# Two layers of attention and Fourier mixing: who issues layer 1's swap transfers, and where VectorE's small tasks stand

## The chip, the cores and the metric

One core of a Trainium2 chip runs the whole program as one launch. The core has a matrix engine (TensorE, PE in the profile, with its weight loads as PEld), a vector engine (VectorE, DVE), an engine for functions of one operand (ScalarE, ACT), a general one (GpSimd, POOL), and one that only issues transfers (SyncE, SP). Each engine takes its instructions in the order in which the program writes them, and waits on semaphores for the others. Matrix results land in PSUM, which has eight banks of 128 x 512 floats.

The metric is the device time in microseconds of one execution. Before the change it was 2400.1 us, the median of three runs (2399.7 to 2401.8).

## The reference

All arrays are float32, with S = 2048 tokens, D = 640 and 32 heads of 20. Two layers follow each other, and each is an attention block and a Fourier block, both with a residual:

```python
def _A_ref(x, wqkv, wo):
    qkv = (x @ wqkv).reshape(B, S, 3, H, Dh).transpose(2, 0, 3, 1, 4)
    q, k, v = qkv[0], qkv[1], qkv[2]
    p = softmax(einsum("bhqd,bhkd->bhqk", q, k) * Dh ** -0.5)
    o = einsum("bhqk,bhkd->bhqd", p, v)
    return o.transpose(0, 2, 1, 3).reshape(B, S, D) @ wo

def _B_ref(x, seq_re, seq_im, hid_re, hid_im):
    a = einsum("bsd,ed->bse", x, hid_re)
    b = einsum("bsd,ed->bse", x, hid_im)
    return einsum("ts,bse->bte", seq_re, a) - einsum("ts,bse->bte", seq_im, b)

x = x + _A_ref(layernorm(x), wqkv, wo)
x = x + _B_ref(layernorm(x), ...)
x = x + _A_ref(layernorm(x), wqkv, wo)     # the same weights again
x = x + _B_ref(layernorm(x), ...)
```

## The kernel before

**Precision.** A float32 product is made of three matmuls in a shorter format: an operand is split into a high part (a copy, rounded) and a low part (the value minus the high part), and high x high, high x low and low x high are added. So every operand costs two elementwise operations: `split` gives the copy to ScalarE (line 93) or VectorE (line 91) and the subtraction to VectorE (line 94).

**The stages of a layer.** A prologue (`Qkv.prologue`, line 370) normalizes the tokens, turns them so that the hidden dimension lies on the partitions, and computes the first chunk of 128 query and of 128 key columns and half of the values, block by block: four blocks (tb) of 512 tokens. Then attention runs over 512 steps (8 groups of four heads, 4 query blocks, 16 key tiles); a step is two score tiles of 128 x 1024, their exponentials, and the products with the values. The other eight chunks of q and k and the other half of the values are computed inside attention, by the generator `work` (line 502). An output projection and the Fourier block end the layer; the end of layer 0's Fourier block is interleaved with the beginning of layer 1's prologue. Whether the layer is the second is what `s.given` says.

**Turning the tokens.** Blocks 0 and 1 are turned by TensorE (`turn`, line 189). Blocks 2 and 3 go another way. `spaced` (line 216) lets ScalarE write the normalized tokens in an order of 4 groups. `swap` (line 225) then lets VectorE transpose each group in squares of 32 x 32 into a tile of its own (line 229, 4 operations, tensor name xz), and 16 transfers (line 232, xs<-xz) bring the squares to their partitions: transfer i of group g reads group g's transposed tile and writes 32 partitions of slab i. The first eight (g = 0, 1) are issued by SyncE, the others by GpSimd. `unspaced` (line 234) splits the result for the matmuls, the copies on ScalarE (xt, line 93). `swap(2)` stands at the end of block 0's work, behind the two `spaced` and ahead of block 1's chunk; `swap(3)` stands in block 1's value tiles, behind the third of four.

**A block of the prologue**, in the program's order: one q chunk and one k chunk, 15 matmuls each (line 111, pqk<-xt,wqk), each followed by `keep` (line 256), where ScalarE makes the high part (hl) and the Square (sq) for a bound on the scores (line 294), VectorE the low part (line 297), and GpSimd stores both to DRAM (line 265); then the matmul of `norms` over the Square of q (line 306, pn<-sq); then four value tiles of 15 matmuls (pv), each evicted by ScalarE (`own`, line 339). Between the value tiles stand the normalizing of the next tokens and `unspaced` of the next block. PSUM's banks go round: `Qkv.bank` (line 185) adds one to `s.n` and takes bank `s.n % 8`. The four value tiles of the last block are the last use before attention lays out its banks anew: three score tiles of two banks each (banks 0 to 5), one bank for the chunks that are still to come and one for the sum over values.

**The order inside attention** is written out by hand as strings. While `work` has chunks left and the step is below 233, a burst of 8 steps follows `DENSE` (line 585). Its letters: s, a score tile and its exponential by ScalarE from PSUM; d, a score tile that VectorE first copies to SBUF (line 688), with its exponential from there; v, the value products of one step; f, a part of a chunk (8 of its 15 matmuls, and at the next f the other 7); n, the norm's matmul of the chunk that is done; h, one place for a small VectorE task. Each of the sixteen value tiles has a shorter string of 4 steps without h.

A place h runs one task of the first of these lists that has any (`step`, line 665): `soon` (what `keep` left: the high part, the low part, the squares; and, when a chunk has had its last block, the next chunk's weights), `ends` (the five operations that finish an accumulator and store it), `held`, and else one task of the constants' comparison. `settle` empties a list at once. The comparison (`Check`, line 988) reads the Fourier matrices through GpSimd's transfers (cq) and checks their symmetries on VectorE, some 26 loads and 200 tasks a layer; `compare` (line 892) hands its tasks out at a pace that runs with the steps, and lets `s.landed` steps pass behind each load before the first task that reads it. All of a layer's comparisons must be out by step 448.

**The weights of the next chunk.** The function `following` (line 522) makes the high and the low part of the next chunk's weights (lines 91 and 94, wqk<-wraw) and fetches the raw weights of the chunk behind it. It is appended to `soon` when the norm's matmul of the chunk's last block is issued, and line 793 settles `soon` there and then inside a burst.

Of the kernel before, what the change touches and what calls it, by code (L numbers as in the profile page):

```python
# [5 lines left out]
F32 = mybir.dt.float32  # L6
F32R = mybir.dt.float32r
# [3 lines left out]
OP = mybir.AluOpType  # L11
# [8 lines left out]
ND = D // 128  # L20
NT = S // 128
NB = S // 512
# [20 lines left out]
def mha_fnet_kernel(ctx, tc, x_in, wqk, wv, wo, seq, hid, nat_seq, nat_hid, out):  # L43
# [107 lines left out]
    class Qkv:  # L151
# [73 lines left out]
        def swap(s, tb):  # L225

            zs = [s.vals(f"v{NT - 1 - g}", [ND * 128], F32, "xz") for g in range(4)]
            for g, z in enumerate(zs):
                V.transpose(z, s.y[tb][:, g].rearrange("p c n f -> p (c n f)"))
            for g, z in enumerate(zs):  # L230
                for i in range(4):
                    (nc.sync if g < 2 else G).dma_start(s.y[tb][32 * g:32 * g + 32, i].rearrange("p c n f -> p (c n f)"), z[32 * i:32 * i + 32])

        def unspaced(s, tb):

# [134 lines left out]
        def prologue(s, vals, xt, fill, att):  # L370
# [42 lines left out]

            def own(tb, n, between=None):
                t = 4 * tb + n
                p = s.bank([128, HD], "pv")
                for dc in range(ND):
                    for f in s.value(p, t, dc):
                        f()
                    if between and dc == 1:  # L420
                        between()
                s.own(p, t, 0, False)
# [79 lines left out]
        def work(s):  # L502

            order = [ND + 1, 1, ND + 2, 2, ND + 3, 3, ND + 4, 4]
            w = {0: s.w1}

            def chunk(i):
                c = order[i]
                for tb in range(NB):
                    p = bank("fill", [128, 512], "pqk")  # L510
                    for more in pieces([s.product(p, w[i], tb, dc) for dc in range(ND)], 8 if (i, tb) < (5, 1) else 5):
                        if more:
                            yield True
                    sq = s.keep(p, c, tb, True, s.fill)

                    def after():
                        s.norms(lambda *a: bank("fill", *a), c, tb, sq)
                        s.made.add((c, tb))
                        if tb == NB - 1:
                            s.made.add(c)  # L520

                            def following():
                                if i + 1 < len(order):
                                    w[i + 1] = s.weights(s.fill("w", [2, ND, 128], F32R, "wqk"), order[i + 1], True)
                                if i + 2 < len(order):
                                    s.fetch(order[i + 2])

                            if s.defer is None:
                                following()
                            else:  # L530
                                s.defer.append(following)
                    yield after

            for i in range(4):
                yield from chunk(i)
            for t in range(NT):
                p = bank("fill", [128, HD], "pv")
                for more in pieces([s.value(p, t, dc) for dc in range(ND)], 15):
                    if more:
                        yield True  # L540
                s.own(p, t, 1, True)
                yield None
            s.made.add("v")
            for i in range(4, 8):
                yield from chunk(i)

            s.silent = True
            r = s.bounds()
            ok = const.tile([128, 1], F32, name="ok", bufs=2)
            V.tensor_scalar(ok[:H], r[:H, 2:3], (GUARD / SCALE) ** 2, None, op0=OP.is_le)  # L550

            def after():
                p = bank("fill", [1, 1], "pok")
                PE.matmul(p, ok[:H], one[:H], start=True, stop=True)
                V.tensor_scalar(s.flag, p, float(H), None, op0=OP.is_equal)
            yield after
# [25 lines left out]
    class Attention:  # L582
        THIN = 233
        LAST = range(448, 512, 16)
        DENSE = "ssdfhhhhsshhsvhvhssvhvssdfhhhhsshhsvhvhssnvv"
        ENDING = "sDsvDhhsfssdvhvssdhvhvsDhsfsDsvhhvsDsvhvsDhsvhvsDhsfsDsvhvhshDshvvv"
        LOOSE = range(THIN, THIN + 176, 16)
        STRING = "sDhsfsDshvvshDsvvshDsfDhsvvsDsvvsDsfshDshvhvsDsvvshDsvhhvsDsnvhv"
# [157 lines left out]
        def sweep(s, shift, begin, fill=lambda n: None, plan=None, block=None, compare=lambda n: None, norm=None):  # L746
# [20 lines left out]
            while n < len(s.steps):  # L767
                opened(n)
                order = plan and plan(n)
                if order:  # L770

                    while done < n - 1:
                        s.values(done)
                        done += 1
                    t, loose = 2 * n, "h" in order
                    for k, c in enumerate(order):
                        if c in "sdD":
                            m, j = divmod(t, 2)
                            if not j and m > n:
                                opened(m)  # L780
                            s.scores(m, j, c)
                            if j and not loose:
                                s.held.append(lambda m=m: compare(m))
                            t += 1
                        elif c == "v":
                            s.values(done)
                            done += 1
                        elif c == "h":
                            s.step(lambda: compare(t // 2 - 1, True))
                        else:  # L790
                            (block if c == "f" else norm if loose else fill)(t // 2)
                            if c == "n" and n < s.THIN:
                                s.settle()
                        if not loose and k + 1 < len(order) and "d" not in order[k + 1:k + 3]:
                            release()
                    n = t // 2
                    continue
                release()
                s.scores(n, 0)
                s.scores(n, 1)  # L800
                more, owed = fill(n) and n >= 2 and n + 1 < len(s.steps), n - 1 - done
                compare(n)
                n += 1
                if plan and n <= s.THIN:
                    count = owed + 1
                elif more and owed < 3:
                    calm = n + 1
                    continue
                else:
                    count = min(owed, 1)  # L810
                    if owed > 1 and (done + 1) % NT and n > calm:
                        calm = n + 1
                        count = 2
                for _ in range(count):
                    s.values(done)
                    done += 1
# [5 lines left out]
        def run(s, done, project, check):  # L822
# [69 lines left out]
            def compare(n, one=False):  # L892
# [4 lines left out]
                for _ in range(1 if one else 2):  # L897
# [2 lines left out]
                        break  # L900
                    task = later.pop(0)
                    if isinstance(task, tuple):
                        s.landed = n + (5 if one else 6)
                        task = task[1]
                    if one:
                        return task()
# [998 lines left out]
```

## Time and profile before

| what | value |
| --- | --- |
| median of three runs | 2400.1 us (2399.7 to 2401.8) |
| the profiled execution's own time | 2400.14 us |
| its span, first to last instruction | 2398.3 us |
| TensorE busy | 2371.0 us, 99% |
| ScalarE busy | 2089.6 us, 87% |
| VectorE busy | 1494.0 us, 62% |
| GpSimd busy | 554.0 us, 23% |
| mean granted TensorE clock | 0.997 |
| layer 0's first scores | at 80.6 us |
| layer 1's prologue, from its first transposes to its first scores | 1197.5 to 1270.2 us |

A busy TensorE isn't a TensorE at its peak, since matmuls are pipelined and the profile models their ends. In the rows of a timeline the columns are the start and the length in microseconds, the engine, the line of the kernel with the operation, what it writes and reads, and how many instructions the row takes together; in brackets stands the idle time of the engine ahead of it and what ended that. A row of the windows has the stretch, its length, the busy time of each engine, the granted clock, and the transfers' share and rate. The groups of the page have the busy time and the mean length of one instruction, and behind the second bar the idle time ahead of the group with what ended it.

### The profile page before, as it was taken

To read this page: it belongs to the slowest core of one execution; us is meant where nothing else is said; L and a number is where in the kernel's file an instruction comes from. 1 tells how busy PE (TensorE), PEld (TensorE's weight loads), DVE (VectorE), ACT (ScalarE), POOL (GpSimd) and SP (SyncE) were. 2 spreads that over 40 slices of the span, in tenths; PEclk is the share of its full clock that TensorE was granted. 3 is DMA by queue.
4 is the path that set the end of the run, shared out by engine and by line. 5 is a ranking of instruction groups with operands and counts; after the bars stand their busy time and mean duration, and the time that the engine had idled before them with its cause. 6 is when DMAs were issued, how large, how long until landed. Compare 5 with 4: busy or idle time off the path is not lost. (4 is left out here: it accounts for less than half of the span.)

```text
span 2398.3 us, 44070 instructions
## 1 busy us (share of the span) xinstructions
PE 2371.0 (99%) x16200; PEld 1170.8 (49%) x16200; DVE 1494.0 (62%) x2747; ACT 2089.6 (87%) x2401; POOL 554.0 (23%) x1080
## 2 busy tenths in 40 slices
PE   9999999999999999999999999999999999999998
PEld 8544445544333332449885444454443333334496
DVE  7355654357777765667773666644567676646675
ACT  5798998899999999995457999988999999999852
POOL 3022221122111222115341122221221111131143
PEclk9999999999999999999999999999999999999999
DMA  6344442223221225219662343432231312242195
GB/s 217 130 140 167 141 135 83 94 96 104 70 78 54 91 72 179 82 30 327 245 225 95 110 128 104 138 102 69 67 96 52 89 49 79 76 136 75 53 336 204
DMA packets 136704, 289.02 MB, mean 121 GB/s; under 512 B 31628, under 2 KB 56108, under 8 KB 136480
## 3 DMA queue, kind: packets, MB, share of 16 engines
q1 hardware_dynamic: 93408, 171.07, 22.0%
q0 software_dynamic: 43072, 115.06, 14.9%
q8 instruction: 130, 2.13, 0.4%
q14 instruction: 94, 0.77, 0.1%
HBM read 187.38 MB, written 92.70 MB: 117 GB/s over the span
## 5 line engine op out<-in xcount | busy, mean ns | idle before, releaser
L691 ACT ACTIVATE e<-psc 128x1024 f32<-128x1024 f32 x1458 | 1448.9, 1130 | 82.7 <-PE psc L683 80.9
L705 PE MATMUL acc<-e,v 128*32 128x512 f32 x7096 | 926.3, 599 | 0.2 <-DVE of L713 0.2
L683 PE MATMUL psc<-stq,stk 62*128 62x512 f32 x4096 | 707.3, 438 | 7.3 <-ACT e L691 3.8
L683 PEld LDWEIGHTS psc<-stq,stk 62*128 62x128 f32 x4096 | 333.7, 184 | 612.5 <-ACT e L691 378.2
L688 DVE COPY e<-psc 128x1024 f32<-128x1024 f32 x316 | 386.2, 1222 | 388.3 <-PE psc L683 364.2
L691 ACT ACTIVATE e<-e 128x1024 f32<-128x1024 f32 x316 | 380.2, 1203 | 7.7 <-DVE e L688 7.7
L705 PEld LDWEIGHTS acc<-e,v 128*32 128x32 f32 x7096 | 202.9, 109 | 366.7 <-issue 322.9
L111 PE MATMUL pqk<-xt,wqk 128*128 128x512 f32 x1200 | 321.7, 408 | 2.9 <-ACT xt L93 0.8
L741 POOL DMA_DIRECT2D o<-oh x256 | 131.1, 519 | 713.5 <-DVE oh L734 690.1
L111 PEld LDWEIGHTS pqk<-xt,wqk 128*128 128x128 f32 x1200 | 213.7, 189 | 96.3 <-issue 44.4
L691 ACT ACTIVATE ex<-psc 128x1024 f32<-128x1024 f32 x136 | 163.0, 1255 | 1.3 <-PE psc L683 1.3
L111 PE MATMUL pv<-wv,xt 128*128 128x320 f32 x960 | 151.7, 313 | 0.0
L111 PEld LDWEIGHTS pv<-wv,xt 128*128 128x128 f32 x960 | 141.0, 188 | 13.7 <-issue 7.6
L705 PE MATMUL acc<-ex,v 128*32 128x512 f32 x856 | 145.6, 598 | 0.0
L741 POOL DMA_DIRECT2D o<-ot x256 | 128.0, 507 | 16.5 <-DVE ot L737 13.7
L688 DVE COPY ex<-psc 128x1024 f32<-128x1024 f32 x78 | 95.5, 1224 | 50.4 <-PE psc L683 44.9
L104 PE MATMUL py<-wo,o 128*128 128x320 f32 x320 | 101.5, 317 | 0.0
L691 ACT ACTIVATE ex<-ex 128x1024 f32<-128x1024 f32 x78 | 101.1, 1296 | 0.0
L1052 DVE TENSOR_REDUCE far<-cq 128x1 f32<-128x512 f32 (+5 forms) x169 | 98.2, 582 | 4.6
L265 POOL DMA_DIRECT2D scrk<-hl x40 | 28.2, 704 | 311.0 <-DVE hl L268 230.9
L106 PE MATMUL py<-wo,o 128*128 128x320 f32 x320 | 98.8, 309 | 0.0
L105 PE MATMUL py<-wo,o 128*128 128x320 f32 x320 | 98.7, 308 | 0.0
(233 smaller groups left out, 2182.9 us busy)
## 6 DMA issues: line engine op xcount, KB each, us to landing
cq<-in_nat_seq_dram POOLq DMA_DIRECT2D x64, 512.0 KB, 5.2
scrq<-hl POOLq DMA_DIRECT2D x40, 512.0 KB, 3.8
scrk<-hl POOLq DMA_DIRECT2D x40, 512.0 KB, 3.2
stq<-scrq SPq DMA_DIRECT2D x256, 80.0 KB
stk<-scrk SPq DMA_DIRECT2D x128, 160.0 KB
chl<-matrix SPq DMA_DIRECT2D x32, 512.0 KB
o<-o SPq DMA_DIRECT2D x32, 384.0 KB
stq<-scrq SPq DMA_DIRECT2D x256, 40.0 KB
```

What stands on the lines that cost most here:

```text
L104: PE.matmul(out_ap, ah, bh, start=start, stop=False)
L105: PE.matmul(out_ap, ah, bl, start=False, stop=False)
L106: PE.matmul(out_ap, al, bh, start=False, stop=stop)
L111: yield lambda i=i, j=j, k=k: PE.matmul(out_ap, a[i], b[j], start=dc == 0 and k == 0, stop=dc == ND - 1 and k == 2)
L265: G.dma_start(s.scr["qk"[k]][c * 128:(c + 1) * 128, :, tb * 512:(tb + 1) * 512], hl.bitcast(F32))
L683: PE.matmul(p[:, i], s.k[g, kc // 8, j][r, kc % 8 * 128:(kc % 8 + 1) * 128], s.q[g, qb, j][r], start=True, stop=True)
L688: V.tensor_copy(e, p)
L691: s.due[n, j] = lambda: A.activation(e, e if copied in ("d", "D") else p, AF.Exp, scale=SCALE)
L705: PE.matmul(s.acc[32 * j:32 * j + 32], s.a.v[kc][:, v0:v0 + 32], s.e[n, j // 2][:, j % 2], start=kc == 0, stop=kc == NT - 1, skip_group_ch ...
L741: G.dma_start(s.o[k, h * DH:(h + 1) * DH, qb * 512:(qb + 1) * 512], hl[32 * j:32 * j + DH])
L1052: V.tensor_reduce(to, x, op=OP.max, axis=AX.X, apply_absolute_value=True)
```

## The change

There are five edits. In layer 1, `swap` gives transfers 0 to 6 to SyncE, 7 to 11 to GpSimd and 12 to 15 to ScalarE; layer 0 keeps its division. In layer 1 the last value tile of the prologue skips ahead to bank 6. The next chunk's weights become two tasks, `high` and `low`, which are appended to `soon` right behind what the last block's `keep` appends; the fetch goes with the second. The settling at n goes. `DENSE` loses one h near its end. The rest behind a load is 6 steps everywhere, where it was 5 for tasks that run in a place h.

```diff
 zs = [s.vals(f"v{NT - 1 - g}", [ND * 128], F32, "xz") for g in range(4)]
 for g, z in enumerate(zs):
     V.transpose(z, s.y[tb][:, g].rearrange("p c n f -> p (c n f)"))
+
+def queue(k):
+    if s.given:
+        return nc.sync if k < 7 else G if k < 12 else A
+    return nc.sync if k < 8 else G
+
 for g, z in enumerate(zs):
     for i in range(4):
-        (nc.sync if g < 2 else G).dma_start(...)
+        queue(4 * g + i).dma_start(...)
...
 def own(tb, n, between=None):
     t = 4 * tb + n
+    if t == NT - 1 and s.given:
+        s.n += (5 - s.n) % 8
     p = s.bank([128, HD], "pv")
...
     sq = s.keep(p, c, tb, True, s.fill)

+    def high():
+        if i + 1 < len(order):
+            w[i + 1] = s.fill("w", [2, ND, 128], F32R, "wqk")
+            V.tensor_copy(w[i + 1][:, 0], s.raw[order[i + 1]])
+
+    def low():
+        if i + 1 < len(order):
+            h = w[i + 1][:, 0].bitcast(F32)
+            V.tensor_tensor(w[i + 1][:, 1], s.raw.pop(order[i + 1]), h, op=OP.subtract)
+        if i + 2 < len(order):
+            s.fetch(order[i + 2])
+
+    following = [high, low]
+    if tb == NB - 1 and s.defer is not None:
+        s.defer += following
+
     def after():
         s.norms(lambda *a: bank("fill", *a), c, tb, sq)
         s.made.add((c, tb))
         if tb == NB - 1:
             s.made.add(c)
-            def following():
-                if i + 1 < len(order):
-                    w[i + 1] = s.weights(s.fill("w", [2, ND, 128], F32R, "wqk"), order[i + 1], True)
-                if i + 2 < len(order):
-                    s.fetch(order[i + 2])
             if s.defer is None:
-                following()
-            else:
-                s.defer.append(following)
+                for f in following:
+                    f()
...
-DENSE = "ssdfhhhhsshhsvhvhssvhvssdfhhhhsshhsvhvhssnvv"
+DENSE = "ssdfhhhhsshhsvhvhssvhvssdfhhhhsshhsvhvssnvv"
...
-                            if c == "n" and n < s.THIN:
-                                s.settle()
...
-                        s.landed = n + (5 if one else 6)
+                        s.landed = n + 6
```

More of the change, by code (lines that the diff above doesn't have):

```diff
@@ L229, in swap @@
                 V.transpose(z, s.y[tb][:, g].rearrange("p c n f -> p (c n f)"))
+            def queue(k):
+                if s.given:
+                    return nc.sync if k < 7 else G if k < 12 else A
+                return nc.sync if k < 8 else G
             for g, z in enumerate(zs):
                 for i in range(4):
-                    (nc.sync if g < 2 else G).dma_start(s.y[tb][32 * g:32 * g + 32, i].rearrange("p c n f -> p (c n f)"), z[32 * i:32 * i + 32])
+                    queue(4 * g + i).dma_start(s.y[tb][32 * g:32 * g + 32, i].rearrange("p c n f -> p (c n f)"), z[32 * i:32 * i + 32])
         def unspaced(s, tb):
```

## The prediction

> **What bounds the kernel now.** I read the page's busy table first, then the ScalarE rows of the timeline through both attentions, then the timeline of every engine through layer 1's prologue (1197 to 1270 us), and last the clock column of the windows. The busy table, and two groups of the page:
>
> ```profile
> span 2398.3 us, 44070 instructions
> PE 2371.0 (99%) x16200; PEld 1170.8 (49%) x16200; DVE 1494.0 (62%) x2747; ACT 2089.6 (87%) x2401; POOL 554.0 (23%) x1080
> ...
> L691 ACT ACTIVATE e<-psc 128x1024 f32<-128x1024 f32 x1458 | 1448.9, 1130 | 82.7 <-PE psc L683 80.9
> ...
> L691 ACT ACTIVATE e<-e 128x1024 f32<-128x1024 f32 x316 | 380.2, 1203 | 7.7 <-DVE e L688 7.7
> ```
>
> TensorE's 99% contains its waits and is no bound by itself. Through attention ScalarE's exponentials set the pace: all that ScalarE waits there is 82.7 us for scores and 7.7 us, in both layers together, for VectorE copies that come late. In the prologues TensorE runs matmul after matmul, and what holds it is paid in full. So the change can act in three places: the 7.7 us, layer 1's prologue, and the step from that prologue into attention.
>
> The 7.7 us. These are ScalarE rows (start, length, instruction, in brackets what it waited before it). The pair of exponentials from PSUM, x2, opens a half burst; the exponential e<-e needs the VectorE copy:
>
> ```profile
> 180.84 1.94 ACT L691 ACTIVATE e<-psc 128x1024 f32<-128x1024 f32 x2 [0.70 <-PE psc L683]
> 189.04 1.94 ACT L691 ACTIVATE e<-psc 128x1024 f32<-128x1024 f32 x2 [0.57 <-PE psc L683]
> 205.41 1.94 ACT L691 ACTIVATE e<-psc 128x1024 f32<-128x1024 f32 x2 [0.57 <-PE psc L683]
> 215.09 1.94 ACT L691 ACTIVATE e<-psc 128x1024 f32<-128x1024 f32 x2 [0.55 <-PE psc L683]
> 279.93 1.94 ACT L691 ACTIVATE e<-psc 128x1024 f32<-128x1024 f32 x2 [0.69 <-PE psc L683]
> 282.79 1.06 ACT L691 ACTIVATE e<-e 128x1024 f32<-128x1024 f32 x1 [0.92 <-DVE e L688]
> 288.61 1.94 ACT L691 ACTIVATE e<-psc 128x1024 f32<-128x1024 f32 x2 [0.20 <-PE psc L683]
> 547.90 1.94 ACT L691 ACTIVATE e<-psc 128x1024 f32<-128x1024 f32 x2 [0.69 <-PE psc L683]
> 556.83 1.94 ACT L691 ACTIVATE e<-psc 128x1024 f32<-128x1024 f32 x2 [0.20 <-PE psc L683]
> 1339.28 1.94 ACT L691 ACTIVATE e<-psc 128x1024 f32<-128x1024 f32 x2 [0.68 <-PE psc L683]
> 1348.31 1.95 ACT L691 ACTIVATE e<-psc 128x1024 f32<-128x1024 f32 x2 [0.20 <-PE psc L683]
> 1470.61 1.94 ACT L691 ACTIVATE e<-psc 128x1024 f32<-128x1024 f32 x2 [0.69 <-PE psc L683]
> 1479.61 1.94 ACT L691 ACTIVATE e<-psc 128x1024 f32<-128x1024 f32 x2 [0.20 <-PE psc L683]
> ```
>
> An undisturbed half burst lasts 189.04 - 180.84 = 8.20 us. The one from 279.93 lasts 8.68: of its wait of 0.92 only 0.48 is lost, because the next wait for scores shrinks from 0.57 to 0.20. In the same way the one from 547.90 loses 8.93 - 8.20 = 0.73, from 1339.28 0.83, from 1470.61 0.80, and the one from 205.41 1.48. What made VectorE late at 282, and at 208:
>
> ```profile
> 279.69 0.47 DVE L91 CAST wqk<-wraw 128x640 fp32r<-128x640 f32 x1
> 280.19 0.83 DVE L94 TENSOR_TENSOR wqk<-wraw,wqk 128x640 fp32r<-128x640 f32 x1
> 280.94 0.71 DVE L713 STREAM_TRANSPOSE of<-acc 128x512 f32<-128x512 f32 x1
> ...
> 207.32 0.43 DVE L1039 CAST cq<-cq 128x512 fp32r<-128x512 f32 x1 [8.41 <-DMA cq<-in_seq_dram]
> ```
>
> The weight split of the next chunk stands between the norm and the finished accumulator's transpose, and the copy comes straight behind the transpose; the half bursts from 547, 1339 and 1470 show the same order. At 207 VectorE stood 8.41 us at a constant that hadn't landed.
>
> Layer 1's prologue, every engine:
>
> ```profile
> 1223.99 0.58 ACT L294 ACTIVATE hl<-pqk 128x512 fp32r<-128x512 f32 x1
> 1224.12 3.02 DVE L229 STREAM_TRANSPOSE xz<-xs 128x640 f32<-128x640 f32 x4 [1.25 <-ACT xs L145]
> 1224.46 0.59 ACT L294 ACTIVATE sq<-pqk 128x512 bf16<-128x512 f32 x1
> 1224.99 5.22 SPq L232 DMA_DIRECT2D xs<-xz  x8
> 1225.55 0.39 PE L306 MATMUL pn<-sq,ind 128*32 128x512 bf16 x1
> 1225.86 9.06 PE L111 MATMUL pv<-wv,xt 128*128 128x320 f32 x60
> ...
> 1232.79 1.74 ACT L145 ACTIVATE xs<-xa,ars 128x640 f32<-128x640 f32 x2 [4.00 <-POOL ars L141]
> 1234.43 0.41 ACT L339 ACTIVATE v<-pv 128x320 f32<-128x320 f32 x1
> 1234.75 2.70 ACT L93 ACTIVATE xt<-xs 128x512 fp32r<-128x512 f32 x5
> 1235.42 0.50 PE L111 MATMUL pqk<-xt,wqk 128*128 128x512 f32 x1 [0.50 <-ACT xt L93]
> 1236.15 6.91 PE L111 MATMUL pqk<-xt,wqk 128*128 128x512 f32 x29 [0.22 <-DVE xt L94]
> 1242.98 0.39 PE L306 MATMUL pn<-sq,ind 128*32 128x512 bf16 x1
> 1252.98 6.91 PE L111 MATMUL pqk<-xt,wqk 128*128 128x512 f32 x29 [0.23 <-DVE xt L94]
> ```
>
> The norm's matmul (1225.55) needs the Square that ScalarE ended at 1224.46 + 0.59 = 1225.05: half a microsecond of slack. The row at 1232.79 shows that ScalarE keeps its order: it stood 4.00 us at one operation with the next eviction behind it.
>
> The step into attention, layer 1 and then layer 0; the row of the windows has the granted clock third from its end:
>
> ```profile
> 1270.23 1.05 PE L683 MATMUL psc<-stq,stk 62*128 62x512 f32 x6 [0.53 <-ACT v L339]
> 1273.26 3.62 PE L111 MATMUL pqk<-xt,wqk 128*128 128x512 f32 x8
> 1277.37 4.75 ACT L691 ACTIVATE e<-psc 128x1024 f32<-128x1024 f32 x5 [1.68 <-PE psc L683]
> 1274.00:1275.00 1.00, 1.00 (x4) 0.71 (x4) 0.59 (x1) 0.98 (x2) 0.00 (x0) 0.50 0.44 139
> ...
> 86.16 4.75 ACT L691 ACTIVATE e<-psc 128x1024 f32<-128x1024 f32 x5 [0.16 <-PE psc L683]
> ```
>
> In layer 1 the first scores wait 0.53 us for the last value tile's eviction, the granted clock falls to 0.50, eight matmuls take 3.62 us, and ScalarE waits 1.68 where layer 0 has 0.16.
>
> **The change, part by part.** *The swap on ScalarE.* Its four transfers (group 3) read the fourth transpose, which ends at 1224.12 + 3.02 = 1227.14, and stand in ScalarE's order ahead of the second token block's eviction and Square. So ScalarE issues from 1227.14 instead of evicting at 1223.99. No ScalarE issue is in the trace; SP takes 5.22/8 = 0.65 us for each of the same transfers, so four cost 2.6. From eviction to the Square's end takes 1225.05 - 1223.99 = 1.06. The Square is done at 1230.8, and TensorE, which can do nothing past the norm's matmul, is held 1230.8 - 1225.55 = **5.25 us**. Behind the hold wait VectorE's low half, GpSimd's store and the value evictions. GpSimd loses three issues net and SP one, but what GpSimd then does waits for the same late eviction: nothing gained. Bounds: SP's shortest row below gives four issues in 1.0 us, a hold of 3.65; issues that alternate with SP's give 7.55 (rivals).
>
> ```profile
> 1264.58 0.26 SPq L575 DMA_DIRECT2D shiftb<-sh  x1
> ```
>
> A hold that long should also drop the clock, as the waits at 1270 did; at that event's price, 1.68 - 0.16 = **1.5** (bounds 0 and, with a second event, 3.0). The later TensorE is, the less it waits further on: 0.50 + 0.22 = **0.72** at the next block comes back.
>
> The second swap: TensorE asks for its Square at 1242.98 + 5.25 + 1.5 - 0.72 = 1249.0. ScalarE has the second value tile of four at about 1230.8 + 0.3 + 9.06/2 + 1.5 = 1237.1, then 0.41 + 2.70 + 1.74 of eviction, splits and normalization to 1242.0, transposes (3.02), issues (2.6), another eviction (0.41) and 1.06: 1249.1. **Nothing** further, since ScalarE is just as late as TensorE (bounds 0 and 2.3). At the fourth block **0.23** comes back, and earlier landings cover nothing more.
>
> *The bank of the last value tile.* It moves from bank 0, which the first scores overwrite, to bank 6, which they don't touch: the **0.53** goes, and with layer 0's pattern of waits the clock should stay up: **1.52** (bounds 0 and 1.52).
>
> *Weights behind keep.* Copy and subtract (0.47 + 0.83 in the rows) run in two of the burst's VectorE places, several places ahead of the norm, and push two comparisons to later bursts. The copy finds VectorE free: 0.48 + 0.73 + 0.83 + 0.80 = **2.84** saved. The fetch behind them is only earlier. If the comparisons fill the hole again, this is 0.
>
> *One place fewer and six steps of rest.* The pattern is used 21 times a layer (16 for the four chunks ahead of the values, 5 behind), so 42 comparisons move to other steps; VectorE is busy 62% of the span, and the comparisons are needed only at the layer's end, so I cost it at nothing (with that cover gone, one more late copy is 0.8 by the rows of 1470). A step more of rest is about 2 us against the 8.41 at 207, so that stall of 1.48 may only move: half of it, **0.74** (bounds 0 and 1.48). The dropped settling finds an empty list, since the norm empties it and the weights are no longer appended there: 0.
>
> Sum: 5.25 + 1.5 - 0.72 - 0.23 - 0.53 - 1.52 = +3.75, and -2.84 - 0.74 = -3.58, together +0.2. On the profiled execution's 2400.14 us (span 2398.3 and 1.84 around it), which stands at the median, 2400.1, this is **2400.3 us: no change**. With the low bounds of the hold and the whole 1.48 it is 3.65 - 0.72 - 0.23 - 2.05 - 4.32 = -3.7, 2396.5; with neither clock saving nor the stall at 207 it is 2402.6.
>
> **Rivals.** *The hold never reaches TensorE* (faster). If ScalarE issues almost free, or something I miss lets the Square pass, the prologue gains the three returned waits and the bank's 2.05, and VectorE's part its 4.32: 0.72 + 0.23 + 2.05 + 4.32 = 7.3, **2392.8**. For it: downstream waits exist to be absorbed. Against it: 1227.14 stands 3.15 us behind the present eviction whatever an issue costs, and the slack is 0.5.
>
> *The issues take turns* (slower). When ScalarE begins, SP still has (1224.99 + 7 x 0.65 - 1227.14)/0.65 = 3.7 issues to make; if both alternate, ScalarE's four end after 7.6 x 0.65 = 4.9 us: a hold of 1227.14 + 4.9 + 1.06 - 1225.55 = 7.55, and at the second swap 2.3 more than TensorE's own lateness covers. 7.55 + 1.5 - 0.72 + 2.3 - 0.23 - 2.05 - 3.58 = +4.8, and one more slow-clock stretch makes +6.3: **2406**. It decides from about 1.2 us an issue. For it: SP is issuing in just that stretch; against it no row speaks, since one engine alone issues this way today. [...]
>
> *VectorE's part isn't what it says*: the displaced comparisons take the places just ahead of the copy and the stalls stay. +3.75 alone: **2403.9**. For it: the list of comparisons is paced and must finish; against it: they need not come before 448 of 512 steps, and what the rows at 279 to 281 show ahead of the copy is the weight split.
>
> [...]
>
> **How the numbers follow.** Forecast 0.45, free hold 0.20, taking turns 0.20, VectorE unchanged 0.15. 0.2% is 4.8 us, about what a measurement of this kernel can tell from no change: the bounds are 2395.3 and 2404.9. Faster: 0.20 and a little of the forecast, 0.23. Slower: most of taking turns and a little of the third, 0.20. The rest, 0.57, is the same. The forecast's own range is 2396.5 to 2402.6; to leave no more than two in ten out, it reaches to 2393 and 2405.5.
>
> **What would show it.** Four issues in ScalarE's row of each layer 1 swap, the first not before 1227.1; a TensorE wait of some 5 us ahead of the norm's matmul in the second block, and slow matmuls behind it; almost none in the third block. No 0.53 at the first scores, and the eight matmuls behind them well under 3.62 us. No weight split directly ahead of an accumulator's transpose; the group e<-e waits 1 to 3 us instead of 7.7. Wrong would be a hold under 2 us, issues over 1.2 us, or late copies at other places.

## The result, and the profile after

The changed kernel takes 2411.94 us (median of six runs, 2409.8 to 2413.56) against 2400.36 us (2398.57 to 2401.8) for the kernel before on the same chip: a ratio of 1.0048 with a 95% interval of 1.0038 to 1.0059. It is slower by 11.6 us; forecast was no change, and 2411.9 lies above the range's upper end, 2405.5. The profiled execution of the changed kernel took 2413.56 us, of which its span is 2411.8: 13.5 us more than the 2398.3 of before. Where a kernel had an execution far above all its others, its ratio and interval leave that one out and its median does not. The lines behind L229 of before have moved by 6 to 17 in the changed kernel: L691 is now L708, L683 is L700, L713 is L730, L306 is L312, L1047 is L1062, L741 is L758; in the experiments' kernels they have moved by 0 to 17.

The page of the changed kernel, the busy table and three groups:

```profile
span 2411.8 us, 44078 instructions
PE 2372.3 (98%) x16200; PEld 1173.8 (49%) x16200; DVE 1496.5 (62%) x2747; ACT 2089.5 (87%) x2401; POOL 551.4 (23%) x1074
...
L708 ACT ACTIVATE e<-psc 128x1024 f32<-128x1024 f32 x1458 | 1449.0, 1115 | 95.1 <-PE psc L700 92.9
L722 PE MATMUL acc<-e,v 128*32 128x512 f32 x7096 | 929.0, 600 | 4.0 <-DVE of L730 3.9
L708 ACT ACTIVATE e<-e 128x1024 f32<-128x1024 f32 x316 | 380.2, 1203 | 0.4 <-DVE e L705 0.2
```

No engine has much more to do than before (VectorE 2.5 us, TensorE 1.3); the loss is waiting and, behind some of the waits, a slower clock (0.993 in the mean, before 0.997). The late copies are gone (e<-e waits 0.4 us, before 7.7), as forecast. But ScalarE waits 95.1 us for scores instead of 82.7, and TensorE, which hardly waited for an accumulator to be taken away before (0.2), now waits 4.0.

To see where, I take one mark that both kernels have 64 times, VectorE's transpose of a finished accumulator (of<-acc, 32 in each layer), and subtract its start before from its start after, by the rows of the timeline. The differences between marks are what each stage gained or lost, in us:

| stage (marks) | after | what it holds |
|---|---|---|
| up to the 1st | +0.7 | layer 0's prologue |
| 1st to 25th | -3.2 | layer 0's attention |
| 25th to 29th | +4.8 | its last steps, about 875 to 995 us |
| 29th to 33rd | +5.7 | layer 1's prologue |
| 33rd to 57th | -2.0 | layer 1's attention |
| 57th to 61st | +6.1 | its last steps, about 2065 to 2185 us |
| behind the 61st | +1.5 | the end |

The prologue and the two dense stretches were in the forecast. The two losses near the end of each attention, 10.9 us together, were not.

**Layer 1's prologue**, the changed kernel's timeline of every engine, and behind it one row of the windows (granted clock 0.50, third from the end):

```profile
1226.53 5.02 SPq L238 DMA_DIRECT2D xs<-xz  x7
1228.76 2.88 ACTq L238 DMA_DIRECT2D xs<-xz  x4
1231.74 0.60 ACT L300 ACTIVATE hl<-pqk 128x512 fp32r<-128x512 f32 x1 [6.12 <-DMA xs<-xz]
1232.88 0.59 PE L312 MATMUL pn<-sq,ind 128*32 128x512 bf16 x1 [5.58 <-ACT sq L300]
1233.40 10.62 PE L111 MATMUL pv<-wv,xt 128*128 128x320 f32 x60
...
1252.17 0.38 PE L312 MATMUL pn<-sq,ind 128*32 128x512 bf16 x1 [1.33 <-ACT sq L300]
...
1234.00:1235.00 1.00, 1.00 (x6) 0.50 0.64 196
```

ScalarE issues four transfers at 0.72 us each, then evicts; the norm's matmul waits 5.58 us for its Square; the sixty matmuls behind it take 10.62 instead of 9.06. The second swap holds its norm 1.33 us. Up to the first scores the prologue lost 5.7 us.

**The step into attention**, TensorE and ScalarE of the changed kernel:

```profile
1278.12 0.97 PE L700 MATMUL psc<-stq,stk 62*128 62x512 f32 x6
1281.12 3.68 PE L111 MATMUL pqk<-xt,wqk 128*128 128x512 f32 x8
1285.27 4.74 ACT L708 ACTIVATE e<-psc 128x1024 f32<-128x1024 f32 x5 [1.73 <-PE psc L700]
```

The wait of 0.53 ahead of the first scores is gone, and yet the eight matmuls are as slow as before (3.68, before 3.62) and ScalarE waits 1.73 (before 1.68).

**The last steps of layer 0**, the changed kernel's queues, VectorE, TensorE and ScalarE, and then the same four of before:

```profile
891.00 0.84 SPq L1222 DMA_DIRECT2D woraw<-in_wo_dram  x2
891.96 0.91 SPq L1240 DMA_DIRECT2D o<-o  x2
892.70 1.47 POOL L1062 DMA_DIRECT2D cq<-in_nat_seq_dram  x2
...
900.18 0.69 DVE L1067 TENSOR_REDUCE ctop<-cq 128x1 f32<-128x512 f32 x1 [4.86 <-DMA cq<-in_nat_seq_dram]
907.01 1.94 PE L722 MATMUL acc<-e,v 128*32 128x512 f32 x8 [2.86 <-DVE of L730]
909.77 1.94 ACT L708 ACTIVATE e<-psc 128x1024 f32<-128x1024 f32 x2 [3.43 <-PE psc L700]
```

```profile
894.17 1.47 POOL L1047 DMA_DIRECT2D cq<-in_nat_seq_dram  x2
894.49 0.84 SPq L1207 DMA_DIRECT2D woraw<-in_wo_dram  x2
895.50 1.35 SPq L1225 DMA_DIRECT2D o<-o  x2
...
900.49 0.69 DVE L1052 TENSOR_REDUCE ctop<-cq 128x1 f32<-128x512 f32 x1 [2.60 <-DMA cq<-in_nat_seq_dram]
906.92 1.07 PE L705 MATMUL acc<-e,v 128*32 128x512 f32 x8 [0.19 <-DVE of L713]
```

Before, GpSimd issued the comparison's load (two transfers of 512 KB) ahead of SP's woraw and o<-o; after, SP's two stand ahead. From its issue the load's comparison starts 900.49 - 894.17 = 6.32 us later before, and 900.18 - 892.70 = 7.48 us after. VectorE stands at it in order, with the comparison's other instructions and then the accumulator's transpose behind it; TensorE waits 2.86 us for that transpose and ScalarE 3.43 for the scores that TensorE then makes. The eight matmuls behind the wait take 1.94 us instead of 1.07: from 906 to 912 us the granted clock is 0.50.

**The last steps of layer 1**, the changed kernel:

```profile
2132.85 1.06 PE L722 MATMUL acc<-e,v 128*32 128x512 f32 x8 [1.07 <-DVE of L730]
2137.71 2.01 POOL L758 DMA_DIRECT2D o<-ot  x4
2139.71 4.40 POOL L1159 DMA_DIRECT2D cq<-in_nat_seq_dram  x8
2143.14 0.41 DVE L1067 TENSOR_REDUCE ctop<-cq 4x1 f32<-4x256 f32 x1 [5.67 <-DMA cq<-in_nat_seq_dram]
2147.15 0.68 DVE L1071 TENSOR_TENSOR cq<-cq 4x512 f32<-4x512 f32 x1 [3.60 <-DMA cq<-in_nat_seq_dram]
2151.81 0.16 PE L1200 MATMUL pflag<-one,cmax 128*1 128x1 f32 x1 [4.79 <-DVE cmax L1195]
2154.59 8.45 ACT L708 ACTIVATE e<-psc 128x1024 f32<-128x1024 f32 x9 [5.37 <-PE psc L700]
```

and before:

```profile
2117.03 4.45 POOL L1144 DMA_DIRECT2D cq<-in_nat_seq_dram  x8 [7.32 <-DVE bound L562]
2135.20 0.17 DVE L1180 TENSOR_REDUCE cmax<-cfar 128x1 f32<-128x22 f32 x1
2138.66 0.16 PE L1185 MATMUL pflag<-one,cmax 128*1 128x1 f32 x1
```

The comparisons do not end on VectorE: their last step is a matmul (pflag) that stands in TensorE's order among the scores of step 441 or 442. Before, VectorE's maximum for it was done at 2135.20 + 0.17 = 2135.37, 3.29 us ahead of TensorE. After, the last load goes out behind a finished accumulator's stores (2137.71), lands at 2143 to 2147, and TensorE waits 4.79 us at the flag, ScalarE 5.37 behind it. The first row is a second, smaller wait in this stage: 1.07 us for an accumulator's transpose.

### The profile page after: what moved, and what is told of

Its sections match the earlier page's. It is cut to its first block, busy times and chain, and to the rows that moved or that the text cites. A ratio compares the mean times of both kernels' runs of the same rounds, so it can differ in the third digit from the quotient of the medians.

```text
span 2411.8 us, 44078 instructions
## 1 busy us (share of the span) xinstructions
PE 2372.3 (98%) x16200; PEld 1173.8 (49%) x16200; DVE 1496.5 (62%) x2747; ACT 2089.5 (87%) x2401; POOL 551.4 (23%) x1074
## 5 line engine op out<-in xcount | busy, mean ns | idle before, releaser
L708 ACT ACTIVATE e<-psc 128x1024 f32<-128x1024 f32 x1458 | 1449.0, 1115 | 95.1 <-PE psc L700 92.9
L700 PE MATMUL psc<-stq,stk 62*128 62x512 f32 x4096 | 705.3, 438 | 6.1 <-ACT e L708 3.9
L700 PEld LDWEIGHTS psc<-stq,stk 62*128 62x128 f32 x4096 | 333.0, 184 | 609.7 <-ACT e L708 377.2
L708 ACT ACTIVATE e<-e 128x1024 f32<-128x1024 f32 x316 | 380.2, 1203 | 0.4 <-DVE e L705 0.2
L758 POOL DMA_DIRECT2D o<-oh x256 | 131.3, 520 | 709.9 <-DVE oh L751 663.0
L708 ACT ACTIVATE ex<-psc 128x1024 f32<-128x1024 f32 x136 | 162.7, 1253 | 1.3 <-PE psc L700 1.3
L758 POOL DMA_DIRECT2D o<-ot x256 | 127.8, 506 | 15.4 <-DVE ot L754 13.3
L708 ACT ACTIVATE ex<-ex 128x1024 f32<-128x1024 f32 x78 | 101.0, 1296 | 0.0
L1071 DVE TENSOR_TENSOR cq<-cq 128x512 f32<-128x512 f32 (+4 forms) x166 | 96.7, 582 | 6.7 <-DMA cq<-in_nat_seq_dram 6.5
```

The lines of the kernel that those rows point to most:

```text
L700: PE.matmul(p[:, i], s.k[g, kc // 8, j][r, kc % 8 * 128:(kc % 8 + 1) * 128], s.q[g, qb, j][r], start=True, stop=True)
L708: s.due[n, j] = lambda: A.activation(e, e if copied in ("d", "D") else p, AF.Exp, scale=SCALE)
L758: G.dma_start(s.o[k, h * DH:(h + 1) * DH, qb * 512:(qb + 1) * 512], hl[32 * j:32 * j + DH])
L1071: V.tensor_tensor(y, x, y, op=op)
```

## The experiments

Each kernel computes all of the reference. Medians and intervals are against runs of the kernel before on the same chip. The stages of each profiled execution are at the end of this section.

**The swap alone.** Edit, in the kernel before:

```
-(nc.sync if g < 2 else G).dma_start(...)
+queue(4 * g + i).dma_start(...)      # layer 1: k < 7 SP, k < 12 GpSimd, else ScalarE
```

> The kernel before with the swap's three queues alone. My theory: the norm's matmul of layer 1's second block is held 5.3 to 5.6 us by ScalarE's four issues (0.7 us each), the 60 matmuls behind it lose another 1.5 us to the clock, and 0.95 us of later waits come back: 2400.4 + 5.3 + 1.5 - 0.95 = 2406.3 us, and the comparisons near step 448 wait as in the kernel before. Rival, the swap also upsets the end of layer 1: 2409 us or more, with ScalarE waits for scores over 1 us near step 448 of layer 1. Rival, later waits absorb the hold: 2403 us or less.

Measured: 2407.28 us against 2399.75; ratio 1.0028, 1.0016 to 1.0040. The end of layer 1 lost nothing, the prologue 7.1 us. TensorE's rows:

```profile
1232.31 0.58 PE L311 MATMUL pn<-sq,ind 128*32 128x512 bf16 x1 [5.60 <-ACT sq L299]
1232.83 11.04 PE L111 MATMUL pv<-wv,xt 128*128 128x320 f32 x60
1252.17 0.38 PE L311 MATMUL pn<-sq,ind 128*32 128x512 bf16 x1 [1.48 <-ACT sq L299]
```

My theory stands: the hold is paid in full (5.60, and 11.04 - 9.06 = 1.98 for the clock), and it has no hand in the losses near step 448.

**The weight split alone.** Edit: high and low behind the keep, the settling dropped.

```
-s.defer.append(following)
+following = [high, low]
+if tb == NB - 1 and s.defer is not None:
+    s.defer += following
```

> The kernel before with the weight split behind the keep (and the settling dropped with it) alone. Theory of quantity (the loss near step 448 comes from comparisons that fewer places and longer rests push to the end): this edit alone takes no place away, so the late copies go, 0.48 + 0.73 + 0.83 + 0.80 = 2.8 us, and nothing is lost: 2397.6 us. Rival, theory of phase (the two places that the split now takes shift what stands ahead of the last accumulators): ScalarE waits for scores near step 448 already here, 2402 to 2408 us.

Measured: 2397.63 us against 2399.75; ratio 0.9989, 0.9980 to 0.9997. The group of the late copies:

```profile
L700 ACT ACTIVATE e<-e 128x1024 f32<-128x1024 f32 x316 | 380.4, 1204 | 1.4 <-DVE e L697 1.2
```

The copies are on time, but layer 0's last steps lost 3.1 us already here; the median is still what the theory of quantity asked for. Neither theory has it all.

**Six steps of rest alone.** Edit:

```
-s.landed = n + (5 if one else 6)
+s.landed = n + 6
```

> The kernel before with six steps of rest behind every comparison load alone. Theory of quantity: each load that rests a step longer leaves more comparisons for the steps up to 448; VectorE then stands 4 us or more at loads there and ScalarE 1 us or more for scores: 2403 to 2406 us. Theory of phase: no change at the end, and half of the 1.48 us at 207 us saved: 2399.7 us.

Measured: 2397.94 us against 2399.75; ratio 0.9991, 0.9982 to 0.9999. No loss near step 448 in either layer; late copies 3.0 us. The theory of quantity missed by 5 us and more, the theory of phase by 1.8.

**One place fewer alone.** Edit: one h out of DENSE (hsvhvhssnvv becomes hsvhvssnvv).

> The kernel before with one VectorE place fewer in the dense pattern alone. Theory of quantity: 42 comparisons move to other steps, some to the last before 448, where they stand ahead of a finished accumulator's transpose: 2402 to 2406 us. Theory of phase: the same comparisons stand at the end as before, 2400.4 us, within 0.1%.

Measured: 2394.99 us against 2399.75; ratio 0.9976, 0.9966 to 0.9986. Neither theory expected that. This part alone takes most of the late copies away; first the group, then ScalarE and VectorE at the place that the prediction showed at 280 us:

```profile
L691 ACT ACTIVATE e<-e 128x1024 f32<-128x1024 f32 x316 | 378.6, 1198 | 1.6 <-DVE e L688 1.4
...
281.18 1.94 ACT L691 ACTIVATE e<-psc 128x1024 f32<-128x1024 f32 x2 [0.69 <-PE psc L683]
281.38 0.71 DVE L713 STREAM_TRANSPOSE of<-acc 128x512 f32<-128x512 f32 x1
```

The weight split still stands straight ahead of the transpose here (L91 at 280.14, L94 at 280.64). But the edit took away the last place ahead of it: the transpose starts 281.38 - 281.18 = 0.20 us behind the start of the pair of exponentials and not 280.94 - 279.93 = 1.01, and the copy behind it isn't late.

So all three VectorE parts gain alone, and by saving from the same 7.7 us: 2.1, 1.8 and 4.8 us by the medians don't add. No part alone shows the loss of layer 1. Following the plan in the code, the comparison loads past step 400 of layer 1 go out at steps 411, 421 and 430 before, and the same with the split alone or one place fewer alone; with six steps of rest alone at 409, 417, 425 and 433; with the split and either of the other two at 410, 418, 426 and 434. The fourth load alone does no harm: with six steps of rest alone it goes out at 2121.75 us, ahead of the accumulator's stores at 2132.09, and nothing is lost. It takes the split and one of the other two for a last load at 434, and in the changed kernel that one goes out behind the stores. In layer 0 the last three stay at 409, 419 and 431 in all of them.

**All but the swap.** Edit, in the changed kernel: the two lines for s.given out of queue.

> The changed kernel with the swap's transfers on two queues as before. My theory, two losses that add: the swap costs what it cost alone, 2407.28 - 2399.75 = 7.5 us by the medians, the waits near step 448 (4.6 us in layer 0, 5.9 in layer 1) stay: 2411.9 - 7.5 = 2404.4 us. Rival, the swap's delay is what puts layer 1's last comparison load out of step: the 5.4 us wait for scores near step 448 of layer 1 goes too, 2398 to 2399 us.

Measured: 2406.78 us against 2400.59; ratio 1.0029, 1.0019 to 1.0038. The losses near step 448 stay (1.8 and 7.0 us): my theory, with the swap worth 2411.9 - 2406.8 = 5.2 us in this company (7.5 alone).

**A shorter rest past step 409.** Edit, in the changed kernel:

```
-s.landed = n + 6
+s.landed = n + (6 if n < 409 else 4)
```

> The changed kernel with four steps of rest instead of six behind the comparison loads from step 409 on. Layer 1's last load then goes out at step 430, as in the kernel before, and not at 434; layer 0's last stays at 431. My theory (layer 1's loss is the last load, issued behind a finished accumulator's stores): the 5.94 us lost there come back and layer 0's 4.6 us stay: 2411.9 - 5.9 = 2406.0 us. Rival, it is the number of comparisons that are left past step 409 and not the last load's place: 2411 to 2413 us, with VectorE at loads that rest too short.

Measured: 2404.65 us against 2400.59; ratio 1.0019, 1.0010 to 1.0029: 7.3 us less than the changed kernel. GpSimd and TensorE in layer 1:

```profile
2117.50 4.48 POOL L1159 DMA_DIRECT2D cq<-in_nat_seq_dram  x8 [6.13 <-DVE bound L579]
2140.13 0.16 PE L1200 MATMUL pflag<-one,cmax 128*1 128x1 f32 x1
```

The last load is ahead of the stores again, TensorE doesn't wait at the flag, and layer 1's last steps lose 0.0 us. This settles layer 1's loss: it is where the loads go out and not how many comparisons are left.

**An earlier end of the comparisons.** Edit, in the changed kernel: pace(s.LAST[0] - 14) for pace(s.LAST[0] - 6).

> The changed kernel with the comparisons paced to end 8 steps earlier. Layer 0's last load goes out at step 426 instead of 431, layer 1's stays at 434. My theory (layer 0's loss is the last load, which lands late behind SP's own transfers): the 4.6 us of layer 0 come back, layer 1's 5.9 stay: 2411.9 - 4.6 = 2407.3 us, and ScalarE's waits of 3.43 and 1.07 at 910 us are gone. Rival, the load is late wherever it goes out, since the DMA engines are full through the whole stretch: 2411 to 2413 us.

Measured: 2413.40 us against 2400.59; ratio 1.0054, 1.0040 to 1.0067. My theory of layer 0 falls. The load that VectorE stands at there isn't the last but the third from the end, the one that the plan hands out at step 409 with either pace; in GpSimd's order it follows the stores of the accumulator ahead of it, and went out no sooner: VectorE waits 4.64 us for it, in the changed kernel 4.86.

**All three mended.** Edit, in the changed kernel: the swap on two queues, the rest of 4 and the earlier pace together.

> The changed kernel with the swap on two queues, four steps of rest past step 409 and the pace of 8 steps earlier: last loads at step 423 in layer 0 and 428 in layer 1. If the three losses add: 2411.9 - 7.5 - 5.9 - 4.6 = 2393.9 us, 0.25% under the kernel before. If they cover each other, 2397 to 2400 us.

Measured: 2409.26 us against 2400.59; ratio 1.0038, 1.0024 to 1.0052, 15 us from the sum. VectorE, TensorE and ScalarE in layer 1:

```profile
2126.31 0.68 DVE L1069 TENSOR_TENSOR cq<-cq 4x512 f32<-4x512 f32 x1 [5.30 <-DMA cq<-in_nat_seq_dram]
2134.63 0.16 PE L1198 MATMUL pflag<-one,cmax 128*1 128x1 f32 x1 [8.91 <-DVE cmax L1193]
2137.40 1.94 ACT L706 ACTIVATE e<-psc 128x1024 f32<-128x1024 f32 x2 [9.49 <-PE psc L698]
```

The earlier pace moved the flag forward in TensorE's order (the list ends at step 434), while VectorE still waited 5.30 us for its load, issued at 2115.20 us: TensorE waits 8.91 us. It is the same wait as in the changed kernel, made larger by moving the other of its two ends. Layer 0's last steps lost 4.9 us again, since the pace doesn't move the load that VectorE stands at there.

**No empty places.** The split leaves two places in VectorE's list behind the last chunk too, where there is nothing to split; they push back the accumulator's steps by two places and bring the shift bound's steps forward. Edit, in the changed kernel:

```
-if tb == NB - 1 and s.defer is not None:
+if tb == NB - 1 and s.defer is not None and i + 1 < len(order):
     s.defer += following
```

> The changed kernel without the two empty places that the weight split leaves behind the last chunk, where nothing follows. VectorE then does the finished accumulator's steps ahead of the shift bound again, as in the kernel before, GpSimd's stores go out earlier and SP's transfers (wo, o<-o) later, behind the comparison's load and not ahead of it. My theory of layer 0's loss: the load lands about 1.2 us sooner after its issue, and ScalarE's wait for scores near 907 us (1.4 to 1.8 us in the runs of this study, 4.5 in the first profile of the changed kernel) goes: 2411.9 - 1.6 = 2410.3 us; layer 1's 6 us stay. Rival, the order of the transfers has no part in it: the wait stays, 2412 us.

Measured: 2409.38 us against 2401.44; ratio 1.0032, 1.0019 to 1.0045: 2.6 us less than the changed kernel, and 3.6 less when each is taken against the kernel before on its own chip (7.9 us above it, the changed kernel 11.6). Layer 0:

```profile
890.49 1.47 POOL L1062 DMA_DIRECT2D cq<-in_nat_seq_dram  x2
891.20 0.84 SPq L1222 DMA_DIRECT2D woraw<-in_wo_dram  x2
896.76 0.69 DVE L1067 TENSOR_REDUCE ctop<-cq 128x1 f32<-128x512 f32 x1 [2.17 <-DMA cq<-in_nat_seq_dram]
```

The load is first again, its comparison starts 6.27 us after its issue, and layer 0's last steps lose 0.0 us. The empty places are the cause there: every kernel of this study that has them loses 1.6 to 4.9 us in that stage, and every one without them 0.1 at most. Two delays add up. The load goes out 19.5 us behind the 25th mark in the six kernels with the empty places and 18.1 to 18.4 us behind it in the eight without; and from its issue to its comparison it takes 7.3 to 9.3 us against 6.0 to 6.4. What the stage then lost went with TensorE's wait and with how fast it ran behind it. In all but the swap and the rest of 4 it waited 2.25 and 1.95 us, the eight matmuls behind took 1.06 us, as before (1.07), and the stage lost 1.8 and 1.7 us; in the three mended it waited 3.89 us and they took 1.62, in the changed kernel 2.86 and 1.94 (granted clock 0.50 from 906 to 912 us), and the stage lost 4.9 and 4.8. The earlier pace lost 1.6 and the split alone 3.1. That the load lands late because it shares the DMA engines with SP's two is what the order of the issues suggests in all of these profiles (in the changed kernel the DMA share is 0.97 from 892 to 900 us); it was not tried by itself. In this profile the last steps of layer 1 lost 8.4 us and not 6.1, so the two stages together gained only 2.5.

**All but the swap, both losses mended.** Edit, in the changed kernel: no empty places, the rest of 4 past step 409, the swap on two queues.

> The changed kernel without the empty places, with four steps of rest past step 409 (layer 1's last load at step 430) and with the swap on two queues: all of the change but the swap, its two losses mended. If the gains and losses measured one by one add: 2411.9 - 5.2 - 7.3 - 1.6 = 2397.8 us. If the late copies' whole 7.7 us come back with nothing lost elsewhere: 2393 to 2394 us. Rival, short rest and VectorE's order bring a new wait near step 448: 2402 us or more.

Measured: 2396.00 us against 2401.44; ratio 0.9980, 0.9971 to 0.9989. The losses add: 2411.9 - 5.2 - 7.3 - 2.6 = 2396.8. Those medians come from different chips; taken each against the kernel before on its own chip, 11.6 - 5.4 - 7.5 - 3.6 = -4.9, measured -5.4.

**One place fewer and the bank.** Edit, in the kernel before: the h out of DENSE, and

```
+if t == NT - 1 and s.given:
+    s.n += (5 - s.n) % 8
```

> The kernel before with one VectorE place fewer and the bank of the last value tile, no other edit. The place alone gave 2395.0 us. If the bank saves only the wait of 0.53 us ahead of the first scores: 2394.5 us. If it also keeps the clock up there, as the prediction had it: 2393 us. The profiles so far speak for the first: the 1.3 to 1.7 us wait for the first scores of layer 1 is there in three of nine and gone in six, in both with and without the bank.

Measured: 2394.40 us against 2401.44; ratio 0.9974, 0.9963 to 0.9984, against 0.9976 without the bank. It has the lowest median of all, below both kernels; what the bank adds can't be told from nothing by these intervals.

**Another group for ScalarE.** Edit, in the swap's kernel: ScalarE if k < 4, SP if k < 11, else GpSimd.

> The kernel before with three queues for layer 1's swap, ScalarE taking transfers 0 to 3 (the first transpose) instead of 12 to 15 (the fourth); SP has 4 to 10, GpSimd 11 to 15. ScalarE then waits for one transpose and not for four, 3 x 0.75 = 2.3 us less, and its four issues take 2.9 us as before. My theory (the hold is the wait for the fourth transpose plus the issues, in ScalarE's order): the norm's matmul of the second block waits 3.3 us instead of 5.6, and the whole is 2399.8 + 7.5 - 2.3 = 2405 us. Rival, the issues themselves slow each other where SP and ScalarE issue at once: the four take over 4 us, and the time stays at 2407 us.

Measured: 2401.20 us against 2401.44; ratio 0.9997, 0.9988 to 1.0006. ScalarE and TensorE:

```profile
1224.31 2.70 ACTq L237 DMA_DIRECT2D xs<-xz  x4
1228.24 0.59 PE L311 MATMUL pn<-sq,ind 128*32 128x512 bf16 x1 [3.12 <-ACT sq L299]
1228.76 10.30 PE L111 MATMUL pv<-wv,xt 128*128 128x320 f32 x60
1245.82 0.39 PE L311 MATMUL pn<-sq,ind 128*32 128x512 bf16 x1
```

The hold fell by 2.48 us, as my theory has it, but the prologue lost only 2.3 us instead of 7.1: with the hold 0.74 of slow clock (11.04 - 10.30) and the second swap's 1.48 went too. The same number of issues by ScalarE, each at 0.7 us; what was dear was the wait for the fourth transpose in ScalarE's order.

What each stage of the profiled execution gained or lost against before, by the same marks as above, with the span's difference last:

| kernel | to 1st | to 25th | to 29th | to 33rd | to 57th | to 61st | behind | span |
|---|---|---|---|---|---|---|---|---|
| changed | +0.7 | -3.2 | +4.8 | +5.7 | -2.0 | +6.1 | +1.5 | +13.5 |
| swap alone | +1.2 | +0.4 | 0.0 | +7.1 | 0.0 | 0.0 | -1.7 | +6.9 |
| split alone | -0.4 | -2.6 | +3.1 | -0.7 | -0.9 | 0.0 | -0.3 | -1.8 |
| rest alone | +1.7 | +0.6 | +0.1 | 0.0 | -1.1 | 0.0 | +1.1 | +2.4 |
| place alone | +2.8 | -2.1 | 0.0 | -1.2 | -1.8 | 0.0 | -1.2 | -3.5 |
| all but the swap | -0.3 | -3.0 | +1.8 | -1.3 | -1.8 | +7.0 | +1.8 | +4.2 |
| rest of 4 | -0.5 | -3.2 | +1.7 | +5.5 | -2.0 | 0.0 | +1.0 | +2.5 |
| earlier pace | +2.9 | -3.2 | +1.6 | +6.0 | -2.0 | +7.0 | +3.0 | +15.1 |
| three mended | +0.1 | -3.0 | +4.9 | -1.2 | -1.9 | +11.6 | +1.2 | +11.8 |
| no empty places | -0.3 | -3.0 | 0.0 | +6.0 | -1.8 | +8.4 | +1.4 | +10.7 |
| all but swap, mended | +1.0 | -3.0 | +0.1 | -2.6 | -1.9 | 0.0 | +1.0 | -5.4 |
| place and bank | +0.2 | -3.1 | 0.0 | -2.0 | -2.0 | 0.0 | -1.3 | -8.3 |
| ScalarE's first group | -0.4 | +0.4 | 0.0 | +2.3 | 0.0 | 0.0 | -1.7 | +0.6 |

The first stage, up to 115 us, and the last differ by 1 to 3 us between executions; the four largest first stages (+1.2 to +2.9) are the four profiles in which the clock fell behind layer 0's first scores. Such a span says which stage changed; how much a kernel gains, the medians say.

## Why the prediction was wrong, step by step

**The step that failed** is the one on one place fewer and six steps of rest: "the comparisons are needed only at the layer's end, so I cost it at nothing". They are needed at step 441 or 442: in layer 1 the list ends in a matmul in TensorE's own order, with 3.29 us of slack before and 4.79 us of wait after. The quoted busy share of VectorE (62% of the span) said nothing about it; the row that would have is TensorE's pflag at 2138.66, 3.3 us behind VectorE's last maximum. With the cover gone I had put 0.8 us, one late copy; it measured 6.1 us in the profile and 7.3 us by the runs. By the plan in the code the split has a part in it: without it, one place fewer and six steps of rest leave the last load at step 433, where rest alone lost nothing (these two together were not run). I looked at what the moved comparisons leave behind and not at where they arrive.

**The weights behind keep**: as forecast, no split stands ahead of an accumulator's transpose any more. But the split was only part of what made the copies late: one place fewer leaves it where it is and takes 7.7 us of waits to 1.6. Missed were the two places that the split takes behind the last chunk for nothing: 4.8 us in the profile of the changed kernel, of which the fallen clock is a part, and 2.6 to 3.6 us by the runs with and without them.

**Late copies**: forecast 2.84 + 0.74 = 3.58 us saved; the dense stretches gained 3.22 + 2.04 = 5.3 us. The terms were undersized, and they were not terms of separate edits: one place fewer alone gains 4.8 us.

**The swap.** Hold 5.25, measured 5.58 in the changed kernel (issue 0.72 us against the 0.65 taken from SP's row); clock behind it 1.5, measured 10.62 - 9.06 = 1.56. Both right. The second swap was put at 0 (bound 2.3); it waits 1.33 us. Returned waits were put at 0.95; at the third block TensorE starts 0.46 us less late than the hold left it, then 0.57, then 0.06 and 0.65 in the next stretches, together 1.74. From the first hold to the first scores the changed kernel loses 5.58 + 1.56 + 1.33 - 1.74 - 0.53 = 6.2 us, and 5.7 with the 0.45 that it came in ahead; forecast to that point 5.27.

**The bank**: the 0.53 went, the 1.52 of clock did not. The slow stretch behind the first scores doesn't need that wait, nor does the wait always bring it. First TensorE and ScalarE of the split alone, with the wait and no slow clock; then of the swap alone, in layer 0, which that edit doesn't touch, with no wait and a slow clock:

```profile
1271.18 1.05 PE L692 MATMUL psc<-stq,stk 62*128 62x512 f32 x6 [0.53 <-ACT v L339]
1276.79 3.84 ACT L700 ACTIVATE e<-psc 128x1024 f32<-128x1024 f32 x4
```

```profile
83.22 3.53 PE L111 MATMUL pqk<-xt,wqk 128*128 128x512 f32 x8
87.33 4.75 ACT L696 ACTIVATE e<-psc 128x1024 f32<-128x1024 f32 x5 [1.68 <-PE psc L688]
```

I had read a cause out of one pair, layer 1 with wait and slow clock against layer 0 with neither. In the fourteen profiles the slow stretch is there in layer 1 in four of the six with the wait and in two of the eight without it, and in layer 0, which never has the wait, in four of fourteen. Whether the wait makes it likelier, so few executions don't show.

**The rivals.** The hold did reach TensorE. The issues did not take turns one for one: SP's went from 0.65 to 5.02/7 = 0.72 us while ScalarE issued at the same rate, and ScalarE's four took 2.88 us, not 4.9. Single ones did stretch, SP's longest of a swap to 1.01 us (before 0.65) and ScalarE's to 0.99. What stretched them no run shows; in SP's mean it is 0.07 us an issue. The 2406 us that this rival gave is the nearest of the totals by luck. VectorE's part did what it says on the copies and something else besides, which none of the rivals named. Summed with what was measured, 2400.1 + 5.7 - 5.3 + 4.8 + 6.1 = 2411.4 and 2.2 us at the first and last stage make the profiled 2413.6.

## What to carry to other kernels

Work that is paced through spare places must be followed to the last thing that uses it, on every engine: ask which instruction of the busiest engine reads its end, and how much slack that one has. A place that is taken for nothing, in an order written out by hand, moves everything behind it, transfers included. And ask when the data of a transfer is there before giving its issue to a busy engine: ScalarE, with the fourth group, stood in its order until that transpose was done (1225.66 + 3.02 = 1228.68 us, first issue at 1228.76), and with the first group it issued from 1224.31 us (nothing measurable by the runs instead of 7.5 us, 2.3 instead of 7.1 in the profiled prologue).

## What the runs showed of the hardware that was not expected

TensorE's clock fell behind ScalarE's first exponentials in some executions and not in others, with the same code and the same waits. In layer 0 ScalarE's wait there is 0.16 us before the change and 0.18 us after it, with a granted clock of 1.00, and 1.68 us in the swap's kernel, where the clock fell to 0.50; TensorE's waits ahead of it are 0.68 and 0.41 us before and 0.68 and 0.42 us in the swap's kernel. Nor does the length of the wait ahead tell by itself. Behind holds of 5.58 and 5.60 us the sixty matmuls took 10.62 and 11.04 us, and behind a hold of 3.12 us, in the kernel with ScalarE's first group, 10.30 - 9.06 = 1.24 us more than before; behind 1.33 us, at the changed kernel's second swap, they took 9.07. And in layer 0 of the swap's kernel the granted clock was 0.50 from 84 to 86 us with no wait of TensorE near it above 0.68 us. What makes it fall these runs don't settle.

The comparison's load of two times 512 KB on GpSimd's queue was usable 6.0 to 6.4 us after its issue in the eight kernels where it went out ahead of SP's transfers, and 7.3 to 9.3 us after it in the six where it went out behind them. That their order is the reason is argued from these profiles and not shown by itself.
